# Joining wo to the down projection along K for token-tile pairs 0 to 6 instead of 1 to 5, with the last pair's products in two other PSUM banks

## Chip, cores, metric

One core of a Trainium2 chip. The metric is the device time of one execution in microseconds (us), lower is better. Engine names in the profile: PE is TensorE's matmuls, PEld its weight loads, DVE is VectorE, ACT is ScalarE, POOL is GpSimd, SP the engine that issues transfers.

## The reference

The output is a residual plus two branches of the same normalised input, for 2048 tokens of width 512:

```python
xn = layernorm(x)
# branch A: linear attention with softmax features, then a projection
o = num / den                       # 2048 x 512
a = o @ wo                          # 512 x 512
# branch B: gated bilinear unit
h = (xn @ w_gate) * (xn @ w_up)     # 2048 x 1792
b = h @ w_down                      # 1792 x 512
out = x + a + b
```

So `wo` and `w_down` both end in the same 512 output columns: `[h, o] @ [w_down; wo]` is one product with a longer K. This is what "joined along K" means.

## The kernel before

Tokens are handled in 8 pairs of 128-token tiles. For a pair the down projection is done by Strassen's scheme in Winograd's form: seven products of half size in place of eight. Each is 7 matmuls along K (half of 1792 is 7 x 128), 128 tokens by 256 columns. The operands are sums of blocks: GpSimd makes four sums of h for every pair (`S1` to `S4`), and the sums of the weights once. There are two forms of the step. The old one adds wo in the plain way:

```python
def DOWN_STEPS(p):                       # cut
    pa, pb = bank(4, 0, 256), bank(5, 0, 256)
    # P1 -> pa, P7 -> pb, P6 -> pa, P5 -> pa: 7 matmuls each
    mm(prod(pb, A22, T4, False) + wo_part(pb, t2, 0), name=f"P4.{p}")     # 7 + 4
    mm(prod(pa, S4, B22, False) + wo_part(pa, t1, 256), name=f"P3.{p}")   # 7 + 4
    mm(prod(d, A12, B21, True) + wo_part(d, t1, 0), name=f"P2.{p}")       # 7 + 4
    # W22: 4 more matmuls of wo in a bank of the ring; in the last pair in two halves
```

The joined form treats wo as two more K blocks of the same scheme, with sums of the attention output oT (`SOSUMS`, on GpSimd, four a pair) and of wo (`TOSUMS`, once):

```python
def CAT_STEPS(p):                        # cut
    def P(n, d, a_, b_, oa, ob, first, last):
        mm(prod(d, a_, b_, first, False), name=f"P{n}.{p}")               # 7
        mm([(d, oa[:, k, :], ob[:, k, :], False, last and k == 1) for k in range(2)],
           name=f"P{n}o.{p}")                                             # + 2
    # order P1 P2 P7 P6 P5 P4 P3; pa holds P1 P6 P5 P3, pb holds P2, then P7 P4
```

After each product VectorE reads the running sum out of the bank, so the next product in that bank has to wait for it. The order of instructions on every engine is fixed at build time by a list scheduler, which takes the first ready step in program order. Beside the pairs TensorE has 28 gate/up units for the last 512 tokens (8 matmuls of 256 columns each, in a ring of banks 0 to 3), and the feature and attention products of the q tiles.

The softmax here doesn't subtract the row's maximum and nothing guards it: scores larger than these inputs give would overflow.

Of the kernel before, what the change touches and what calls it, by code (L numbers as in the profile page):

```python
# [16 lines left out]
D = 512  # L17
# [342 lines left out]
PD = -1  # L360
PX = -1
SE = {}
UE = 1.6
QP0 = 1
QP1 = 2
# [2 lines left out]
TRQ = 1500.0  # L368
TRO = 800.0
PS = -1  # L370
CAT = (1, 2, 3, 4, 5)
SOE = POOL
TOE = POOL
PLN = 0
# [12 lines left out]
def _build(nc, es, A_x, A_wqkv, A_w_phi, A_wo, B_w_gate, B_w_up, B_w_down, out):  # L387
# [65 lines left out]
    def bank(b, lo=0, n=512):  # L453
        return psum[:, b * 512 + lo: b * 512 + lo + n]
# [67 lines left out]
    def group(o, pairs):  # L522
        n = len(pairs)
        return [(o, l, r, i == 0, i == n - 1) for i, (l, r) in enumerate(pairs)]
# [15 lines left out]
    def xnT(q, s_lo, n):  # L540
        return xnT_v[:, q, s_lo:s_lo + n]
# [250 lines left out]
    def hs(s_lo):  # L792
        return s_lo % 1536
# [76 lines left out]
    def BLOCK(kind, ft, ba):  # L870
# [58 lines left out]
                act_op(gslot(ft, 2), pa, name=f"ge{ft}.2", prio=PA)  # L929
        return [p1, p7, p6, p2, p4, p5, p3]  # L930

    def U2(ft, s_lo):
        b = nb()
        mm(group(bank(b, 0, 256), [(wg_v[:, q, ft * 128:(ft + 1) * 128], xnT(q, s_lo, 256)) for q in range(NQ)])
           + group(bank(b, 256, 256), [(wu_v[:, q, ft * 128:(ft + 1) * 128], xnT(q, s_lo, 256)) for q in range(NQ)]),
           name=f"gu{ft}.{s_lo}")
        g = gring()[:, 0:256]
        act_op(g, bank(b, 0, 256), name=f"ge{ft}.{s_lo}")
        h = hT_v[:, ft, hs(s_lo):hs(s_lo) + 256]
        dve(lambda e: e.tensor_tensor(out=h, in0=bank(b, 256, 256), in1=g, op=ALU.mult), [bank(b, 256, 256), g], [h],  # L940
            name=f"h{ft}.{s_lo}")

    def GU2(fts, s_lo, bg, bu, order):
# [48 lines left out]
    def NUM(t):  # L992
        nv = numb()
        mm([(nv[:, c, 0:68], qT_v[:, t % NQT, c, :], kvbd_v[:, c, :], True, True) for c in range(8)], name=f"n{t}")
        sm = qsum_v[:, t % 5, :].rearrange("p (c h s) -> p c h s", c=8, s=2)[:, :, :, 0]
        w = qw_v[:, t % 4, :]
        wv4 = w.rearrange("p (c h) -> p c h", c=8)
        den = nv[:, :, 64:68]
        dve(lambda e: e.scalar_tensor_tensor(out=wv4, in0=sm, scalar=1e-6, in1=den, op0=ALU.mult, op1=ALU.add),
            [qsum_v[:, t % 5, :], den], [w], cost=210.0, name=f"nd{t}")  # L1000
        dve(lambda e: e.reciprocal(out=w, in_=w), [w], [w], cost=360.0, name=f"nr{t}")  # L1001
        o = oslot(t)
        ov = o.rearrange("p (c h d) -> p c h d", c=8, h=4)
        src = nv[:, :, 0:64].rearrange("p c (h d) -> p c h d", h=4)
        dve(lambda e: e.tensor_tensor(out=ov, in0=src, in1=wv4[:, :, :, None].to_broadcast([128, 8, 4, 16]),  # L1005
                                      op=ALU.mult), [src, w], [o], cost=600.0, name=f"no{t}")
        dst = oT_v[:, t % 4, :, :]
        sc.dma(SP, dst, o, 131072, turn=True, reads=[o], writes=[dst], name=f"oT{t}").reserve = TRO
# [17 lines left out]
    def hA(half, t):  # L1026
        s = hs(t * 128)
        return hT_v[:, half * HF:(half + 1) * HF, s:s + 128]

    def SSUMS(p):  # L1030
        assert ui[0] >= (10 if p < 2 else NA2 if p < 6 else NA2 + (14, 28)[p - 6])
        S1, S2, S3, S4 = (S_v[:, p % 2, w] for w in range(4))
        A11, A12, A21, A22 = hA(0, 2 * p), hA(1, 2 * p), hA(0, 2 * p + 1), hA(1, 2 * p + 1)
        e3, e1, e2, e4 = (DVE if c == "D" else POOL for c in SE.get(p, "PPPP"))
        sums(e3, S3, A11, A21, ALU.subtract, f"S3.{p}", 0)
        sums(e1, S1, A21, A22, ALU.add, f"S1.{p}", 0)
        sums(e2, S2, S1, A11, ALU.subtract, f"S2.{p}", 0)
        sums(e4, S4, A12, S2, ALU.subtract, f"S4.{p}", 0)

    To_v = sbv("x", 12 * 512, 4 * 512).bitcast(F16).rearrange("p (w k j) -> p w k j", w=4, k=2)  # L1040
    So_v = sbv("vext", 0, 2 * 4 * 256).bitcast(F16).rearrange("p (r w k s) -> p r w k s", r=2, w=4, k=2)
# [37 lines left out]
    def DOWN_STEPS(p):  # L1079
        t1, t2 = 2 * p, 2 * p + 1  # L1080
        final = p == NT // 2 - 1
        S1, S2, S3, S4 = (S_v[:, p % 2, w] for w in range(4))
        A11, A12, A22 = hA(0, t1), hA(1, t1), hA(1, t2)
        pa, pb = bank(4, 0, 256), bank(5, 0, 256)
        t11, t21, t22 = (tf_v[:, p % 2, w] for w in range(3))

        def o(t, c):
            return sbv("ostg", (t % 4) * 512 + c * 256, 256)

        def x(t, c):  # L1090
            return x_res(t)[:, c * 256:(c + 1) * 256]

        def s1():
            mm(prod(pa, A11, B11, True), name=f"P1.{p}")
            post(p, t11, pa, x(t1, 0), "t11")

        def s2():
            mm(prod(pb, S3, T3, True), name=f"P7.{p}")
            post(p, t22, pb, x(t2, 1), "t22")

        def s3():
            mm(prod(pa, S2, T2, False), name=f"P6.{p}")
            post(p, t21, pa, x(t2, 0), "t21")

        def s4():
            mm(prod(pa, S1, T1, False), name=f"P5.{p}")
            post(p, t22, pa, t22, "t22b")

        def s5():
            mm(prod(pb, A22, T4, False) + wo_part(pb, t2, 0), name=f"P4.{p}")  # L1110
            post(p, o(t2, 0), pb, t21, "c21")
            if p == NT // 2 - 1:
                store(t2, 0, 256)

        def s6():
            mm(prod(pa, S4, B22, False) + wo_part(pa, t1, 256), name=f"P3.{p}")
            post(p, o(t1, 1), pa, x(t1, 1), "c12")
            if p == NT // 2 - 1:
                store(t1, 256, 256)

        def s7():
            d = bank(nb(), 0, 256) if final else pb
            mm(prod(d, A12, B21, True) + wo_part(d, t1, 0), name=f"P2.{p}")
            post(p, o(t1, 0), d, t11, "c11")
            store(t1, 0, 256 if p == NT // 2 - 1 else 512)

        def s8():
            w = 128 if final else 256
            for lo in range(0, 256, w):
                d = bank(nb(), 0, w)  # L1130
                mm([(d, oT_v[:, t2 % 4, q, :], wo_v[:, q, 256 + lo:256 + lo + w], q == 0, q == NQ - 1)
                    for q in range(NQ)], name=f"W22.{p}")
                oo, tt = o(t2, 1)[:, lo:lo + w], t22[:, lo:lo + w]
                dve(lambda e, oo=oo, d=d, tt=tt: e.tensor_tensor(out=oo, in0=d, in1=tt, op=ALU.add), [d, tt], [oo],
                    cost=60.0 + 1.045 * w, name=f"c22.{p}.{lo}")
            if final:
                store(t2, 256, 256, ACT)
            else:
                store(t2, 0, 512)
        if final:  # L1140
            return [s1, s2, s3, s4, s7, s5, s6, s8]
        return [s1, s2, s3, s4, s5, s6, s7, s8]

    def CAT_STEPS(p):
# [2 lines left out]
        S1, S2, S3, S4 = (S_v[:, p % 2, w] for w in range(4))  # L1147
        O1, O2, O3, O4 = (So_v[:, p % 2, w] for w in range(4))
        R1, R2, R3, R4 = (To_v[:, w] for w in range(4))
        A11, A12, A22 = hA(0, t1), hA(1, t1), hA(1, t2)  # L1150
        pa, pb = bank(4, 0, 256), bank(5, 0, 256)
        t11, t21, t22 = (tf_v[:, p % 2, w] for w in range(3))

        def o(t, c):
# [8 lines left out]

        def s1():
            P(1, pa, A11, B11, oA(0, t1), oB(0, 0), True, False)
            post(p, t11, pa, x(t1, 0), "t11")

        def s2():
            P(2, pb, A12, B21, oA(1, t1), oB(1, 0), True, True)
            post(p, o(t1, 0), pb, t11, "c11")  # L1170

        def s3():
            P(7, pb, S3, T3, O3, R3, True, False)
# [15 lines left out]
        def s7():  # L1189
            P(3, pa, S4, B22, O4, oB(1, 1), False, True)  # L1190
            post(p, o(t1, 1), pa, x(t1, 1), "c12")
            store(t1, 0, 512)
        return [s1, s2, s3, s4, s5, s6, s7, lambda: None]

    one = nc.const_aps.tensor(1.0, [128, 512], BF16)

# [48 lines left out]
    rest = [(U, f, sg) for ft in range(NB, NF // 2) for f in (ft, ft + NF // 2) for sg in (1, 2)]  # L1245
    units += rest
    NA2 = len(units)
    units += [(U2, ft, s_lo) for s_lo in (1536, 1792) for ft in range(NF)]
    ui = [0]

    def nextU():
        if ui[0] < len(units):
# [44 lines left out]
    assert ui[0] >= NA  # L1297
    load_x(SP, 4, 4, name="rx")
    load_x(SP, 8, 4, name="rx")
    down = DOWN_STEPS(0)  # L1300
    nextU()
    KVS(NT, 1)
    KVX()
    ring_banks[0] = [0, 1, 2, 3]
    rp[0] = 0
    nextU()
    down[0]()
    down[1]()
    NUM(0)
    nextU()  # L1310
    SSUMS(1)
    nextU()
    NUM(1)
    TOSUMS(TOE)
    u0 = ui[0]
    n_left = len(units) - u0
    NP = NT // 2
    for p in range(NP):
        def some(fr):
            k = int(round(u0 + n_left * min(1.0, (p + fr) / (NP - UE))))  # L1320
            while ui[0] < min(k, len(units)):
                nextU()
        a, b = 2 * p + 2, 2 * p + QA
        if p == 2:
            load_x(SP, 12, 4, name="rx", slot=0)
        def Qs(pos):
            for k, at in ((0, QP0), (1, QP1)):
                if at == pos and b + k < NT:
                    Q(b + k)
        if p > 0:  # L1330
            down = CAT_STEPS(p) if p in CAT else DOWN_STEPS(p)
            Qs(0)
            down[0]()
            some(0.1)
            Qs(1)
            down[1]()
# [8 lines left out]
        some(0.4)  # L1345
        Qs(3)
        down[3]()
        if 2 <= p + 1 < NP:
            SSUMS(p + 1)
        if a + 1 < NT:  # L1350
            NUM(a + 1)
# [7 lines left out]
        some(0.8)  # L1359
        down[6]()  # L1360
        some(1.0)
        down[7]()

    assert ui[0] == len(units)
    sc.chain("P6.7 P2.7 P5.7 P4.7 P3.7")

    for st in sc.steps:
        if st.eng in (ACT, DVE, POOL) and not isinstance(st.lane, tuple) and st.idx > late[0]:
# [40 lines left out]
```

## Time and profile before

| | before |
|---|---|
| median of 3 runs | 211.93 us (211.37 to 212.01) |
| span of the core in the profiled run | 209.8 us |
| PE busy | 204.5 us, 97% |
| GpSimd busy | 169.6 us, 81% |
| weight loads (one a matmul, all recorded) | 1620 |

How to read it: the page gives each engine's busy time and share. PE's ends are modelled, so 97% alone does not show that it never waits. The lines themselves stand in the prediction below.

### The profile page before, as it was taken

Reading aid. Unit: us, or ns where it says so; the run is one execution under the profiler, and the core shown is the slowest. Engines: PE = TensorE matmul, PEld = TensorE weight load, DVE = VectorE, ACT = ScalarE, POOL = GpSimd, SP = SyncE. Lnnn points to the kernel's source line nnn. Section 1 sums busy time; section 2 is a strip of 40 time slices with the busy share of each in tenths; the row PEclk is TensorE's granted clock in tenths of the full one; section 3 lists DMA queues with packets and bytes.
Section 4 is the critical chain, followed back from the end, with each engine's and each line's share of the span. In section 5 each row is a group of like instructions: output and inputs, shape, how many; then the busy total and the mean of one; then the engine's idle time right before and its main releaser. Section 6 shows DMA issues by size and latency. Waiting matters only on the chain.

```text
span 209.8 us, 4274 instructions
## 1 busy us (share of the span) xinstructions
PE 204.5 (97%) x1603; PEld 136.3 (65%) x1620; DVE 158.7 (76%) x307; ACT 113.3 (54%) x293; POOL 169.6 (81%) x215
## 2 busy tenths in 40 slices
PE   8999999999999999999999999999999999999995
PEld 3875444444454444454456797988978888799884
DVE  4857799998966797989987875948659486695743
ACT  4756999698796959697822613416144251531000
POOL 4061698439999999999999999999999989990540
PEclk9999999999999999999999999999999999999999
DMA  5999924964100000222521135183351705635211
GB/s 161 334 264 355 245 59 96 327 137 140 32 18 0 3 0 0 50 52 53 197 54 28 25 78 125 34 174 101 70 129 25 175 13 115 80 75 128 50 52 50
DMA packets 50244, 21.52 MB, mean 103 GB/s; under 512 B 37424, under 2 KB 50224, under 8 KB 50224
## 3 DMA queue, kind: packets, MB, share of 16 engines
q1 hardware_dynamic: 49552, 20.93, 40.5%
q10 hardware_dynamic: 672, 0.33, 0.6%
q8 instruction: 12, 0.20, 0.4%
q14 instruction: 8, 0.07, 0.1%
HBM read 10.24 MB, written 2.10 MB: 59 GB/s over the span
## 4 chain that ended last, share of the span: by engine, by line
PE 80%; POOL 7%; ACT 5%; DMA 3%; DVE 2%; issue 1%; DVEq 0%
PE ps L510 78%; ACT arena L463 5%; POOL arena L781 4%; DMA arena<-arena 3%; PE ps L1199 2%; POOL arena L731 2%; POOL arena L636 1%; DVE arena L781 1%; DVE arena L722 1%; POOL arena L729 0%; DVE arena L756 0%; ACT ps L463 0%; DVE arena L940 0%; DVE arena L1071 0%; DVEq L349 0%
## 5 line engine op out<-in xcount | busy, mean ns | idle before, releaser
L510 PE MATMUL ps<-arena 128*128 128x256 bf16 (+5 forms) x1593 | 200.3, 286 | 1.9 <-ACT ps L463 0.4
L510 PEld LDWEIGHTS ps<-arena 128*128 128x128 bf16 (+1 forms) x1610 | 135.0, 98 | 67.8 <-ACT arena L463 2.0
L781 POOL TENSOR_TENSOR arena<-arena 128x256 f16<-128x256 bf16 (+3 forms) x120 | 124.3, 1060 | 12.9 <-DVE arena L940 7.4
L463 ACT ACTIVATE arena<-ps 128x512 bf16<-128x512 f32 (+3 forms) x168 | 83.4, 533 | 67.9 <-PE ps L510 64.7
L722 DVE TENSOR_REDUCE arena<-arena 128x64 f32<-128x1024 bf16 x32 | 38.6, 1208 | 1.0 <-ACT arena L463 0.9
L1071 DVE TENSOR_TENSOR arena<-ps,arena 128x256 bf16<-128x256 f32 (+1 forms) x56 | 23.3, 422 | 17.4 <-PE ps L510 16.1
L463 ACT ACTIVATE arena<-arena 128x64 f32<-128x64 f32 (+4 forms) x96 | 28.4, 314 | 12.2 <-DVE arena L722 8.8
L731 POOL TENSOR_TENSOR arena<-arena 128x512 bf16<-128x512 bf16 x32 | 33.8, 1060 | 0.4
L940 DVE TENSOR_TENSOR arena<-ps,arena 128x256 f16<-128x256 f32 x30 | 12.4, 420 | 11.3 <-ACT arena L463 9.7
L862 DVE TENSOR_TENSOR arena<-ps,arena 128x512 f16<-128x512 f32 x24 | 16.1, 683 | 1.0 <-PE ps L510 0.8
L811 DVE TENSOR_TENSOR arena<-ps,arena 128x512 f16<-128x512 f32 x14 | 9.5, 684 | 4.9 <-PE ps L510 3.5
L756 DVE TENSOR_TENSOR arena<-ps,arena 128x512 bf16<-128x512 f32 x16 | 10.8, 683 | 2.1 <-ACT arena L463 1.5
L627 DVE BATCH_NORM_STATS2 arena<-arena 128x6 f32<-128x512 bf16 x16 | 10.5, 673 | 2.1 <-DMA arena<-in_A_x_dram 2.0
L868 DVE TENSOR_TENSOR ps<-ps,arena 128x512 f32<-128x512 f32 x12 | 8.2, 696 | 4.3 <-PE ps L510 3.0
L1005 DVE TENSOR_TENSOR arena<-ps,arena 128x512 bf16<-128x512 f32 x16 | 11.0, 685 | 0.3
L729 POOL TENSOR_TENSOR arena<-arena 128x32 f32<-128x32 f32 x32 | 8.3, 262 | 3.5 <-ACT arena L463 3.4
L609 POOL TENSOR_TENSOR arena<-arena 128x128 bf16<-128x128 bf16 x4 | 1.6, 428 | 8.7 <-DMA arena<-in_A_w_phi_dram 8.7
L636 POOL TENSOR_SCALAR arena<-arena 128x1 f32<-128x1 f32 x12 | 3.3, 290 | 6.0 <-ACT arena L463 6.0
L868 DVE TENSOR_TENSOR arena<-ps,arena 128x512 bf16<-128x512 f32 x12 | 8.0, 680 | 0.0
L463 ACT ACTIVATE ps<-ps 128x512 f32<-128x512 f32 x12 | 7.2, 600 | 0.0
L1001 DVE RECIPROCAL arena<-arena 128x32 f32<-128x32 f32 x16 | 5.6, 352 | 0.5
L1199 PE MATMUL ps<-const-bfloat16-1.0 128*128 128x512 bf16 x10 | 4.4, 626 | 0.8 <-PEq L1394 0.8
(22 smaller groups left out, 26.6 us busy)
## 6 DMA issues: line engine op xcount, KB each, us to landing
arena<-in_A_x_dram SPq DMA_DIRECT2D x6, 512.0 KB, 5.2
arena<-in_B_w_down_dram SPq DMA_DIRECT2D x1, 1792.0 KB, 7.6
out_dram<-arena SPq DMA_DIRECT2D x14, 128.0 KB, 2.0
arena<-in_B_w_gate_dram SPq DMA_DIRECT2D x1, 768.0 KB, 7.9
arena<-in_B_w_up_dram SPq DMA_DIRECT2D x1, 768.0 KB, 8.4
arena<-arena SPq DMA_TRANSPOSE x44, 2.5
arena<-in_B_w_gate_dram SPq DMA_DIRECT2D x2, 256.0 KB, 4.4
arena<-in_B_w_gate_dram SPq DMA_DIRECT2D x1, 512.0 KB, 6.1
```

The costliest lines, as they stand in the source:

```text
L463: return e.activation(out=out_ap, in_=in_ap, func=func, scale=scale, **kw)
L510: ins = e.matmul(o, lhsT=l, rhs=r, start=s, stop=p, skip_group_check=True)
L627: dve(lambda e, t=t: e.bn_stats(stats_v[:, t, :], x_tile(t)), [x_tile(t)], [stats_v[:, t, :]], cost=600.0, name=f"st{t}", win=win, prio=prio)
L722: dve(lambda e, ei=ei, so=so: e.tensor_reduce(out=so, in_=ei.rearrange("p (h f) -> p h f", f=16), axis=AX.X, op=ALU.add), [ei], [so], cost ...
L731: pool(lambda e: e.tensor_tensor(out=ev[:, :, 1, :], in0=ev[:, :, 1, :], in1=ratio[:, :, None].to_broadcast([128, H, 16]), op=ALU.mult), [ ...
L756: dve(lambda e: e.tensor_tensor(out=o1, in0=src, in1=rp_[:, :, :, None].to_broadcast([128, 8, 4, 16]), op=ALU.mult), [src, rs_v[:, t % 4, ...
L781: fn = lambda e: e.tensor_tensor(out=out_, in0=a_, in1=b_, op=op)
L862: dve(lambda e: e.tensor_tensor(out=h, in0=src, in1=g, op=ALU.mult), [src, g], [h], name=f"h{ft}.{sg}", prio=PD)
L868: dve(lambda e: e.tensor_tensor(out=o, in0=src, in1=sn, op=ALU.add), [src, sn], [o], name=name, prio=PD)
L940: dve(lambda e: e.tensor_tensor(out=h, in0=bank(b, 256, 256), in1=g, op=ALU.mult), [bank(b, 256, 256), g], [h], name=f"h{ft}.{s_lo}")
L1005: dve(lambda e: e.tensor_tensor(out=ov, in0=src, in1=wv4[:, :, :, None].to_broadcast([128, 8, 4, 16]), op=ALU.mult), [src, w], [o], cost=6 ...
L1071: dve(lambda e: e.tensor_tensor(out=out_, in0=in_ps, in1=in_sb, op=ALU.add), [in_ps, in_sb], [out_], cost=328.0, name=f"{name}.{p}")
```

## The change

The intent is to save the matmuls that the plain form of wo costs more, in two more pairs, and to give the last pair's first products banks that are free before pair 6 is done. The core of the diff:

```diff
-CAT = (1, 2, 3, 4, 5)
+CAT = (0, 1, 2, 3, 4, 5, 6)
+AB = {7: (2, 3)}
 ...
-        pa, pb = bank(4, 0, 256), bank(5, 0, 256)
+        pa, pb = (bank(b, 0, 256) for b in AB.get(p, (4, 5)))
 ...
-    down = DOWN_STEPS(0)
+    down = CAT_STEPS(0) if 0 in CAT else DOWN_STEPS(0)
 ...
-    down[0]()
-    down[1]()
+    if 0 not in CAT:
+        down[0]()
+        down[1]()
     NUM(0)
 ...
     TOSUMS(TOE)
+    if 0 in CAT:
+        SOSUMS(0, SOE)
+        SSUMS(1)
+        down[0]()
+        down[1]()
 ...
+        if p in AB:
+            ring_banks[0] = [0, 1]
```

The rest adds settings that are off (other orders, Strassen blocks for the gate/up units at count 0) and exchanges the halves of a bank in which the late gate/up units keep gate and up.

More of the change, by code (lines that the diff above doesn't have):

```diff
@@ L362 @@
 SE = {}
+SED = 'PPPP'
+SLATE = ()
+P2B = ()
+AB = {7: (2, 3)}
+CO = {}
+CH = "P6.7 P2.7 P5.7 P4.7 P3.7"
+NX = 0
+ZP = 0
+WSE = POOL
+XSE = POOL
+PB = -1
+NRA = ()
+SD = ()
+SPL = ((0, 7),)
 UE = 1.6
@@ L930, in BLOCK @@
         return [p1, p7, p6, p2, p4, p5, p3]
+    Tz_v = xnT_v[:, :, 0:512].bitcast(F16).rearrange("p w (k s) -> p w k s", k=2)
+    zw = [sbv("Wp", NQ * 512, 1024), sbv("Wp", NQ * 512 + 1024, 1024), sbv("wv", NQ * 512 - 1024, 1024)]
+    zw = [v.bitcast(F16).rearrange("p (w k j) -> p w k j", w=4, k=2) for v in zw]
+    zs = sbv("sums", 0, 1024).bitcast(F16).rearrange("p (r s) -> p r s", r=4)
+    zg = sbv("gring", 0, 4 * 512).rearrange("p (r s) -> p r s", r=8)
+    zc = {"w": 0, "s": 0, "g": 0}
@@ new lines, in _build, with zB, ZXSUMS, ZWSUMS @@
+    zgate = {}
+    zW = {}
+    def zB(k, c):
+        return xnT_v[:, 2 * k:2 * k + 2, 1536 + c * 256:1792 + c * 256]
+    def ZXSUMS():
+        X1, X2, X3, X4 = (Tz_v[:, w] for w in range(4))
+        for n, (o_, a_, b_) in enumerate(((X1, zB(0, 1), zB(0, 0)), (X3, zB(1, 1), zB(0, 1)), (X2, zB(1, 1), X1),
+                                          (X4, zB(1, 0), X2))):
+            sums(XSE, o_, a_, b_, ALU.subtract, f"Xz{n}", 0)
+    def ZWSUMS(kind, ft):
+        zW[kind, ft] = zw[zc["w"] % 3]
+        zc["w"] += 1
+        S1, S2, S3, S4 = (zW[kind, ft][:, w] for w in range(4))
+        A = lambda i, k: wA(W_v[kind], i, k, ft)
+        sums(WSE, S3, A(0, 0), A(1, 0), ALU.subtract, f"{kind}z3.{ft}", 0)
+        sums(WSE, S1, A(1, 0), A(1, 1), ALU.add, f"{kind}z1.{ft}", 0)
+        sums(WSE, S2, S1, A(0, 0), ALU.subtract, f"{kind}z2.{ft}", 0)
+        sums(WSE, S4, A(0, 1), S2, ALU.subtract, f"{kind}z4.{ft}", 0)
@@ new lines, in zsnap, with zgslot, ZBLOCK, S @@
+    def zsnap():
+        zc["s"] += 1
+        return zs[:, zc["s"] % 4, :]
+    def zgslot(f, c):
+        zc["g"] += 1
+        zgate[f, c] = zg[:, zc["g"] % 8, :]
+        return zgate[f, c]
+    def ZBLOCK(kind, ft):
+        ft2 = ft + NF // 2
+        A = lambda i, k: wA(W_v[kind], i, k, ft)
+        X1, X2, X3, X4 = (Tz_v[:, w] for w in range(4))
+        st = {}
+        nm = f"z{kind}.{ft}"
+        def S(w):
+            return zW[kind, ft][:, w]
+        def take(k):
+            st[k + "i"] = nb(True)
+            st[k] = bank(st[k + "i"], 0, 256)
+            return st[k]
+        def free(k):
+            held.discard(st[k + "i"])
+        def zadd(o_, a_, b_, n):
+            dve(lambda e: e.tensor_tensor(out=o_, in0=a_, in1=b_, op=ALU.add), [a_, b_], [o_], cost=328.0,
+                name=n + nm, prio=PB)
+        def done(f, c, src):
+            if kind == "g":
+                act_op(zgslot(f, c), src, name=f"ge{nm}", prio=PB)
+                return
+            h = hT_v[:, f, hs(1536 + c * 256):hs(1536 + c * 256) + 256]
+            g = zgate[f, c]
+            dve(lambda e: e.tensor_tensor(out=h, in0=src, in1=g, op=ALU.mult), [src, g], [h], cost=328.0,
+                name=f"h{nm}", prio=PB)
+        def p1():
+            pa = take("a")
+            xprod(pa, A(0, 0), zB(0, 0), True, "b1" + nm)
+            seed(take("c"), pa, "sd" + nm)
+        def p7():
+            pb = take("b")
+            xprod(pb, S(2), X3, True, "b7" + nm)
+            st["p7"] = zsnap()
+            act_op(st["p7"], pb, name="s7" + nm, prio=PB)
+        def p2():
+            xprod(st["c"], A(0, 1), zB(1, 0), False, "b2" + nm)
+            done(ft, 0, st["c"])
+            free("c")
+        def p6():
+            xprod(st["a"], S(1), X2, False, "b6" + nm)
+            st["u2"] = zsnap()
+            act_op(st["u2"], st["a"], name="s2" + nm, prio=PB)
+        def p4():
+            pb = st["b"]
+            xprod(pb, A(1, 1), X4, False, "b4" + nm)
+            if kind == "g":
+                zadd(zgslot(ft2, 0), pb, st["u2"], "a4")
+            else:
+                zadd(pb, pb, st["u2"], "a4")
+                done(ft2, 0, pb)
+            free("b")
+        def p5():
+            xprod(st["a"], S(0), X1, False, "b5" + nm)
+            if kind == "g":
+                zadd(zgslot(ft2, 1), st["a"], st["p7"], "a5")
+            else:
+                pt = bank(nb(), 0, 256)
+                zadd(pt, st["a"], st["p7"], "a5")
+                done(ft2, 1, pt)
+        def p3():
+            xprod(st["a"], S(3), zB(1, 1), False, "b3" + nm)
+            done(ft, 1, st["a"])
+            free("a")
+        return [p1, p7, p2, p6, p4, p5, p3]
@@ L932, in U2 @@
     def U2(ft, s_lo):
         b = nb()
-        mm(group(bank(b, 0, 256), [(wg_v[:, q, ft * 128:(ft + 1) * 128], xnT(q, s_lo, 256)) for q in range(NQ)])
-           + group(bank(b, 256, 256), [(wu_v[:, q, ft * 128:(ft + 1) * 128], xnT(q, s_lo, 256)) for q in range(NQ)]),
+        GLO = 256 if s_lo >= 1536 else 0
+        mm(group(bank(b, GLO, 256), [(wg_v[:, q, ft * 128:(ft + 1) * 128], xnT(q, s_lo, 256)) for q in range(NQ)])
+           + group(bank(b, 256 - GLO, 256), [(wu_v[:, q, ft * 128:(ft + 1) * 128], xnT(q, s_lo, 256)) for q in range(NQ)]),
@@ L936, in U2 @@
            name=f"gu{ft}.{s_lo}")
         g = gring()[:, 0:256]
-        act_op(g, bank(b, 0, 256), name=f"ge{ft}.{s_lo}")
+        act_op(g, bank(b, GLO, 256), name=f"ge{ft}.{s_lo}")
         h = hT_v[:, ft, hs(s_lo):hs(s_lo) + 256]
-        dve(lambda e: e.tensor_tensor(out=h, in0=bank(b, 256, 256), in1=g, op=ALU.mult), [bank(b, 256, 256), g], [h],
+        dve(lambda e: e.tensor_tensor(out=h, in0=bank(b, 256 - GLO, 256), in1=g, op=ALU.mult), [bank(b, 256 - GLO, 256), g], [h],
             name=f"h{ft}.{s_lo}")
@@ L1000, in NUM @@
             [qsum_v[:, t % 5, :], den], [w], cost=210.0, name=f"nd{t}")
-        dve(lambda e: e.reciprocal(out=w, in_=w), [w], [w], cost=360.0, name=f"nr{t}")
+        if t in NRA:
+            recip(w, w, f"nr{t}")
+        else:
+            dve(lambda e: e.reciprocal(out=w, in_=w), [w], [w], cost=360.0, name=f"nr{t}")
         o = oslot(t)
@@ L1030, in SSUMS @@
     def SSUMS(p):
-        assert ui[0] >= (10 if p < 2 else NA2 if p < 6 else NA2 + (14, 28)[p - 6])
+        assert ui[0] >= (10 if p < 2 else NA2 if p < 6 else (NA3, len(units))[p - 6])
         S1, S2, S3, S4 = (S_v[:, p % 2, w] for w in range(4))
         A11, A12, A21, A22 = hA(0, 2 * p), hA(1, 2 * p), hA(0, 2 * p + 1), hA(1, 2 * p + 1)
-        e3, e1, e2, e4 = (DVE if c == "D" else POOL for c in SE.get(p, "PPPP"))
-        sums(e3, S3, A11, A21, ALU.subtract, f"S3.{p}", 0)
-        sums(e1, S1, A21, A22, ALU.add, f"S1.{p}", 0)
-        sums(e2, S2, S1, A11, ALU.subtract, f"S2.{p}", 0)
-        sums(e4, S4, A12, S2, ALU.subtract, f"S4.{p}", 0)
+        es = [DVE if c == "D" else POOL for c in SE.get(p, SED)]
+        for (n, o_, a_, b_, op), eng in zip(((3, S3, A11, A21, ALU.subtract), (1, S1, A21, A22, ALU.add),
+                                             (2, S2, S1, A11, ALU.subtract), (4, S4, A12, S2, ALU.subtract)), es):
+            for lo, hi in SPL if eng == POOL else ((0, HF),):
+                sums(eng, o_[:, lo:hi], a_[:, lo:hi], b_[:, lo:hi], op, f"S{n}.{p}" + (f".{lo}" if lo else ""), 0)
     To_v = sbv("x", 12 * 512, 4 * 512).bitcast(F16).rearrange("p (w k j) -> p w k j", w=4, k=2)
@@ L1121, in s7 @@
         def s7():
-            d = bank(nb(), 0, 256) if final else pb
+            d = bank(nb(), 0, 256) if final or p in P2B else pb
             mm(prod(d, A12, B21, True) + wo_part(d, t1, 0), name=f"P2.{p}")
@@ L1149, in CAT_STEPS @@
         R1, R2, R3, R4 = (To_v[:, w] for w in range(4))
+        cb = []
         A11, A12, A22 = hA(0, t1), hA(1, t1), hA(1, t2)
-        pa, pb = bank(4, 0, 256), bank(5, 0, 256)
+        pa, pb = (bank(b, 0, 256) for b in AB.get(p, (4, 5)))
         t11, t21, t22 = (tf_v[:, p % 2, w] for w in range(3))
@@ L1165, in s1 @@
             P(1, pa, A11, B11, oA(0, t1), oB(0, 0), True, False)
-            post(p, t11, pa, x(t1, 0), "t11")
-        def s2():
-            P(2, pb, A12, B21, oA(1, t1), oB(1, 0), True, True)
-            post(p, o(t1, 0), pb, t11, "c11")
+            if p in SD:
+                cb.append(nb(True))
+                seed(bank(cb[0], 0, 256), pa, f"sd11.{p}")
+            else:
+                post(p, t11, pa, x(t1, 0), "t11")
+        def s2():
+            if p in SD:
+                d = bank(cb[0], 0, 256)
+                P(2, d, A12, B21, oA(1, t1), oB(1, 0), False, True)
+                post(p, o(t1, 0), d, x(t1, 0), "c11")
+                held.discard(cb[0])
+                return
+            d = bank(nb(), 0, 256) if p in P2B else pb
+            P(2, d, A12, B21, oA(1, t1), oB(1, 0), True, True)
+            post(p, o(t1, 0), d, t11, "c11")
         def s3():
@@ L1192, in s7 @@
             store(t1, 0, 512)
-        return [s1, s2, s3, s4, s5, s6, s7, lambda: None]
+        order = CO.get(p, "1276543")
+        f = {"1": s1, "2": s2, "7": s3, "6": s4, "5": s5, "4": s6, "3": s7}
+        return [f[c] for c in order] + [lambda: None]
     one = nc.const_aps.tensor(1.0, [128, 512], BF16)
@@ L1247, in _build, with weight @@
     NA2 = len(units)
-    units += [(U2, ft, s_lo) for s_lo in (1536, 1792) for ft in range(NF)]
+    std = [ft for ft in range(NF) if ft % (NF // 2) >= NX]
+    units += [(U2, ft, 1536) for ft in std]
+    blocks = [(kind, ft) for ft in range(NX) for kind in "gu"]
+    for i, b in enumerate(blocks):
+        units += [(f,) for f in ZBLOCK(*b)]
+        if i + 3 < len(blocks):
+            units.append((ZWSUMS,) + blocks[i + 3])
+    NA3 = len(units)
+    units += [(U2, ft, 1792) for ft in std]
     ui = [0]
+    def weight(u):
+        return 4 if u[0] is U2 or u[0] is U else 0 if u[0] is ZWSUMS else 1
     def nextU():
@@ L1306, in _build @@
     nextU()
-    down[0]()
-    down[1]()
+    if 0 not in CAT:
+        down[0]()
+        down[1]()
     NUM(0)
     nextU()
-    SSUMS(1)
+    if 0 not in CAT:
+        SSUMS(1)
     nextU()
@@ L1314, in _build @@
     TOSUMS(TOE)
+    if 0 in CAT:
+        SOSUMS(0, SOE)
+        SSUMS(1)
+        down[0]()
+        down[1]()
+    cum = [0]
+    for u in units[ui[0]:]:
+        cum.append(cum[-1] + weight(u))
     u0 = ui[0]
-    n_left = len(units) - u0
     NP = NT // 2
@@ L1319, in some @@
         def some(fr):
-            k = int(round(u0 + n_left * min(1.0, (p + fr) / (NP - UE))))
-            while ui[0] < min(k, len(units)):
+            k = cum[-1] * min(1.0, (p + fr) / (NP - UE))
+            while ui[0] < len(units) and cum[ui[0] - u0] + weight(units[ui[0]]) / 2 <= k:
                 nextU()
+        if p == ZP and NX:
+            ZXSUMS()
+            for b_ in blocks[:3]:
+                ZWSUMS(*b_)
         a, b = 2 * p + 2, 2 * p + QA
@@ L1347, in _build @@
         down[3]()
-        if 2 <= p + 1 < NP:
+        if 2 <= p + 1 < NP and p + 1 not in SLATE:
             SSUMS(p + 1)
@@ L1361, in _build @@
         some(1.0)
+        if p + 1 in SLATE:
+            SSUMS(p + 1)
         down[7]()
     assert ui[0] == len(units)
-    sc.chain("P6.7 P2.7 P5.7 P4.7 P3.7")
+    sc.chain(CH)
     for st in sc.steps:
```

## The prediction

> **What bounds the kernel now.** I read the page first, then the waits of TensorE, the groups by form, the busy time by stretch, and last the chain of waits and the timelines of the end. The top of the page says which engine the time belongs to:
>
> ```profile
> span 209.8 us, 4274 instructions
> PE 204.5 (97%) x1603; PEld 136.3 (65%) x1620; DVE 158.7 (76%) x307; ACT 113.3 (54%) x293; POOL 169.6 (81%) x215
> PE   8999999999999999999999999999999999999995
> POOL 4061698439999999999999999999999989990540
> PEclk9999999999999999999999999999999999999999
> ```
>
> TensorE (PE) is occupied nearly everywhere at a full clock; GpSimd (POOL) is full from slice 10 to slice 36, and has holes only in the last four slices. A busy PE could still hide waits, so the next question is what PE waited for:
>
> ```profile
> PE ps L1199 <- PEq L1394: 0.8, 1, 0.8
> PE ps L510 <- ACT ps L463: 0.4, 1, 0.4
> PE ps L510 <- DVE arena L868: 0.3, 1, 0.3
> PE ps L510 <- issue: 0.2, 1, 0.2
> PE ps L510 <- ACT arena L463: 0.2, 1, 0.2
> ```
>
> Columns: who waited for whom, total us, times, longest. That is 1.9 us in the whole run, and none of it in the part that the change touches. The chain of waits (start us, length us, what) confirms it:
>
> ```profile
> 179.22 0.05 issue
> 179.27 27.60 PE ps L510 x267
> 206.87 0.02 issue
> 206.89 0.42 DVE arena L1071
> 207.31 0.20 DVE arena L1134
> 207.51 0.20 DVEq L349
> ```
>
> From 57 us on the chain is PE alone, back to back; after its last product there are about 2.5 us of last additions and the last store. So in the down-projection stage (about 109 to 207 us) the time is the number of matmuls times the spacing of one, as long as nothing makes PE wait. The spacing comes from a stretch that holds only 256-column matmuls (columns: window, length, busy us and count for PE, PEld, DVE, ACT, POOL, clock, DMA share, GB/s):
>
> ```profile
> 190.00:197.00 7.00, 7.00 (x78) 6.32 (x77) 4.78 (x14) 1.15 (x3) 0.91 (x1) 1.00 0.39 94
> 197.00:206.00 9.00, 9.00 (x85) 8.05 (x83) 4.61 (x11) 0.00 (x0) 4.74 (x3) 1.00 0.18 53
> ```
>
> Every matmul has one weight load, and all 1620 weight loads are recorded while some matmul records are missing; so 9.00 us / 83 = 108.4 ns a matmul. By counting weight loads in program order I also matched them to the products: product P6 of the last pair takes 7 matmuls in 0.75 us, P2 with its four of wo 1.2 us for 11, which is the same spacing.
>
> **What the Trainium skill says.** "TensorE: Matmul & The Clock Gate", Back-to-back issue gap, gives N/2.4 + 2.5 ns for a warm stream: 109.2 ns at N = 256. The trace agrees (108.4). "PSUM — Partial Sum Buffer", Terms, says that two engines on one bank at once are an error, so each read of an accumulator by VectorE must be a wait for the next product in that bank; the trace shows the length of this turn: P1 of pair 6 ends at 191.33, its VectorE read runs 191.64 to 192.07, so about 0.8 us with the signal back. "GPSIMD Engine Reference", 3.1 Elementwise, puts a two-input elementwise at about 2.6 cycles an element, which at 1.2 GHz is 2.2 ns; here 896 elements take 1883 ns (2.1 ns) and 256 take 673 ns (a fixed part shows), so it agrees roughly and I use the durations. "DMA: Bandwidth & Descriptors", Anatomy of one DMA, has about 2.0 us fixed; the transposes that bring the attention output oT take 2.3 us from issue to landing.
>
> **The change, part by part.** *TensorE.* Both forms do seven half-size products (Strassen's scheme) of 7 matmuls along K, 49 in all. The old form adds wo plainly: 4 matmuls in P4, P3 and P2 and a block W22 of 4, so 16, total 65. The joined form adds two matmuls to each product: 14, total 63. Two fewer a pair, two pairs (0 and 6): 4 x 108.4 ns = **0.43 us less** PE work. Pair 7 stays in the old form.
>
> *VectorE.* The old form has 8 additions a pair, the joined 7: two fewer of about 0.42 us, 0.84 us, beside PE.
>
> *GpSimd.* Each newly joined pair needs four sums of oT:
>
> ```profile
> L781 POOL TENSOR_TENSOR arena<-arena 128x896 f16<-128x896 f16 x32 | 60.1, 1883 | 11.3 <-DVE arena L940 7.4 <-DMA arena<-arena 3.4 <-PE ps L510 0.2
> L781 POOL TENSOR_TENSOR arena<-arena 128x256 f16<-128x256 bf16 x55 | 36.2, 673 | 1.5 <-DMA arena<-in_B_w_up_dram 1.4
> ```
>
> 8 x 0.67 = 5.4 us more, 2.7 at pair 0 and 2.7 at pair 6. The four sums of wo (1.16 us each) exist already, but pair 0 now needs them, and they move ahead of the sums of pair 1.
>
> *Pair 0.* Its old P1 and P7 ran at 109.1 to 110.5 without oT. Now P1 and P2 come first, P7 third, and every product has an oT part. oT of tile 0 landed at 114.82, of tile 1 at 118.77. GpSimd can then give the four sums between about 119 and 123; the old P4 of this pair ran at 120.7 and the pair ended at 125.8, so the need is at about the same time. Gate/up units stand ready as other PE work (28 of them, 8 matmuls or 0.87 us each, none bound to this pair's oT). The 2.7 us push back the GpSimd queue, but what it pushes is early: the second sum for pair 2 is done at 129.3 and its product runs near 148; the sums of pair 6 are done at 183 and used from 193. The short margin is the sums of oT of pair 1 (third sum done 133.0, used 133.6), which are placed ahead of the large sums in the queue. I count 0.
>
> *Pair 6.* Its sums of oT wait for tile 13, landed at 189.97; GpSimd sits idle there:
>
> ```profile
> 187.59 1.06 POOL L731 TENSOR_TENSOR arena<-arena 128x512 bf16<-128x512 bf16 x1
> 196.09 5.80 POOL L781 TENSOR_TENSOR arena<-arena 128x896 f16<-128x896 f16 x3 [7.45 <-DVE arena L940]
> ```
>
> (start us, length us, engine, line, ..., idle before). Four sums fit from 190 to 193 in the 7.45 us hole, before the sums of pair 7 at 196.1. I count 0 if they don't slip.
>
> *The other banks.* Joined pair 6 has P2 and P7 in one bank, with a VectorE read between, and P6 and P5 in the other: two turns of 0.8 us which need other PE work. After the last gate/up unit (194.86) only one small attention product and pair 7 are left. In banks 4 and 5 the first two products of pair 7 would have to wait for pair 6; in banks 2 and 3 they can be that filler (2 x 0.76 us). So the bank change mostly keeps the 0.43 us from being lost; by itself it can save nothing, since PE does not wait there today.
>
> *The rest of the diff* (new knobs, Z blocks at zero count, gate and up halves of a bank exchanged in the late units) changes no number of instructions.
>
> Sum: 211.93 - 0.43 = **211.5 us**.
>
> **The rivals.** *A. GpSimd becomes the bound.* For: it is at 81%, full for two thirds of the run, and gets 5.4 us. If the 2.7 us at pair 0 were passed on, the time would be up to 211.9 + 2.3 = 214.2. Against: PE waits for it nowhere after 109 us but at a margin of 10 us and more for the large sums, and from 170 us on it has small holes that absorb the delay. *B. A new wait in the last pairs.* The second sum of pair 7 is done at 199.9 and its product starts at 201.47, a margin of 1.5 us; with 0.43 us less PE work before it, 1.1 us is left. If the sums of pair 6's oT, or a gate/up unit run later by 1 us, eat this, PE waits and the gain is gone: 211.9 to 212.5. For: this is where fillers are few. *C. More than the count.* If the exchange of banks and order also removed small waits, 210.8; against: 0.05 us pieces of "issue" every ten us are all that the chain shows to remove, plus one turn at the very end that stays.
>
> **Range and chances.** The central value is C's neighbour, the plain count. The runs of before spread from 211.37 to 212.01, as much as the whole effect, so the range is 0.7 us either side: 210.8 to 212.2, with B inside and A outside. Two per cent is 4.2 us, ten times the gain: faster 0.01, same 0.97, slower 0.02 (A at its worst plus a wait at the end).
>
> **What would show it.** The changed profile should have 1616 weight loads, two VectorE additions fewer, 219 to 223 GpSimd instructions (8 more) and about 175 us of it; PE's waits still near 1.9 us; the span about 0.4 us shorter, all of it between 109 and 207 us; the 7.45 us hole of GpSimd split in two around a group of four sums of 256; P1 and P7 of pair 7 mixed into pair 6. I am wrong on A if PE shows waits for POOL from 115 to 135 us; on B if one appears after 195 us; and if the weight loads fall by 4 with the spacing unchanged and the span does not follow, the price was a wait that the views must name.

## The result, and the profile after

| | before | changed |
|---|---|---|
| median | 211.97 us, 6 runs (211.01 to 212.22) | 210.95 us, 6 runs (210.67 to 211.42) |
| span of the profiled run | 209.8 us | 209.6 us |
| weight loads | 1620 | 1616 |
| VectorE / GpSimd instructions | 307 / 215 | 305 / 223 |

The ratio is 0.9963, 95% interval 0.9939 to 0.9988. Ratios here are the mean time of one kernel's fast runs over that of the other's of the same rounds, so not quite the ratio of the medians. The class is "same", as forecast, and the time lies inside the stated range; but the ratio means 0.8 us, and the prediction had worked out 0.43. The experiments ask which of the two is the change.

The top of the page after:

```profile
span 209.6 us, 4281 instructions
PE 205.6 (98%) x1616; PEld 136.3 (65%) x1616; DVE 158.5 (76%) x305; ACT 113.9 (54%) x293; POOL 174.5 (83%) x223
PE   8999999999999999999999999999999999999995
POOL 4070598439999999999999999999999999997640
```

The instruction counts moved exactly as the two forms say. PE's busy time went up although it has four matmuls fewer: this trace has every matmul record (1616), that of before lacks 17, so busy PE is not to be compared between the two. GpSimd is now full up to slice 36 and its holes at the end are smaller. What PE waited for, and the end of the chain of waits (start us, length us, what):

```profile
PE ps L1345 <- PEq L1568: 0.8, 1, 0.8
PE ps L524 <- ACT ps L477: 0.4, 1, 0.4
PE ps L524 <- DVE arena L882: 0.3, 1, 0.3
```

```profile
57.45 149.26 PE ps L524 x1252
206.71 0.02 issue
206.73 0.42 DVE arena L1203
207.15 0.20 DVE arena L1266
207.35 0.20 DVEq L349
```

No wait is new, and the chain from 57 us on is one piece of PE. The weight loads say the same more sharply; the timeline of PEld from 107 us on has one row, before and after, which means no idle time of 150 ns or more until the last product (columns: start, length, engine, line, operation, out<-in, count, idle time before):

```profile
106.91 100.21 PEld L510 LDWEIGHTS ps<-arena 128*128 128x128 bf16 x952
```

```profile
107.14 99.83 PEld L524 LDWEIGHTS ps<-arena 128*128 128x128 bf16 x950 [0.32 <-DVE arena L770]
```

So where did the time come from? All weight loads are recorded in both traces, so counting them in program order names every product; the start and end times of single products below were found in this way. I take as **the stage** the stretch from the end of the last k-v product (the last thing that both programs have in the same place on PE: the first 200 steps on PE are the same, and so are the first 40 transfers that SP issues) to the end of the last wo block. As windows of before, and of the changed kernel (length first, then busy us and counts for PE, PEld, DVE, ACT, POOL):

```profile
109.15:207.12 97.97, 97.65 (x928) 82.12 (x930) 67.21 (x150) 29.85 (x79) 83.92 (x77) 1.00 0.37 80
```

```profile
109.42:206.96 97.54, 97.54 (x931) 81.73 (x927) 66.96 (x148) 30.29 (x79) 88.77 (x85) 1.00 0.39 80
```

97.97 against 97.54: 0.43 us, the four matmuls. The counts in these two lines include the records that straddle the window's edges. The profiled run of the changed kernel reached the stage 0.27 us later (109.42 against 109.15), in a part where the programs do not differ; that is why the two spans differ by only 0.2 us.

### The profile page after: what moved, and what is told of

The parts are those of the page before. It is cut to its first block, busy times and chain, and to the rows that moved or that the text cites. A ratio compares the mean times of both kernels' runs of the same rounds, so it can differ in the third digit from the quotient of the medians.

```text
span 209.6 us, 4281 instructions
## 1 busy us (share of the span) xinstructions
PE 205.6 (98%) x1616; PEld 136.3 (65%) x1616; DVE 158.5 (76%) x305; ACT 113.9 (54%) x293; POOL 174.5 (83%) x223
## 4 chain that ended last, share of the span: by engine, by line
PE 81%; POOL 7%; ACT 5%; DMA 3%; DVE 2%; issue 1%; DVEq 0%
PE ps L524 79%; ACT arena L477 5%; POOL arena L795 4%; DMA arena<-arena 3%; PE ps L1345 2%; POOL arena L745 2%; DVE arena L795 1%; POOL arena L650 1%; DVE arena L736 1%; POOL arena L743 0%; ACT ps L477 0%; DVE arena L1203 0%; DVEq L349 0%; DVE arena L1266 0%; ACT arena L773 0%
## 5 line engine op out<-in xcount | busy, mean ns | idle before, releaser
L795 POOL TENSOR_TENSOR arena<-arena 128x256 f16<-128x256 bf16 (+3 forms) x128 | 129.4, 1034 | 7.5 <-DMA arena<-arena 3.4
```

The costliest lines, as they stand in the source:

```text
L795: fn = lambda e: e.tensor_tensor(out=out_, in0=a_, in1=b_, op=op)
```

## The experiments

Theory A: the change is worth its four matmuls, and the new banks are what keeps this from being lost to waits. Theory B: something beyond the count gained, since the timed runs show about 0.8 us. A third view, a rival of both: GpSimd is so near its bound that its extra sums decide. The stage is measured in each profiled run, beside the timed ratio with its interval. Each run had 5 rounds, with the kernel before run beside it. All outputs were correct.

### 1. The changed kernel again, twice

No edit. First:

> The changed kernel once more, unaltered. If the saving is only the four matmuls (theory A: 4 x 108.4 ns = 0.43 us), the ratio to before is about 0.998 and its interval should hold 0.998; in the trace the stretch from the end of the last k-v product (kv15) to the end of the last wo block is 0.4 to 0.5 us shorter than before's, and what differs ahead of kv15 is run to run. If something beyond the count helped (theory B, since the medians on record differ by 1.0 us), the ratio is 0.995 again and the stretch after kv15 is shorter by 0.8 us or more.

Measured: 211.11 us against 211.84, ratio 0.9958 (0.9932 to 0.9984). The stage is 97.54 us, before it 109.04. And:

> The changed kernel a third time, beside the one above on the same chip. The stretch after kv15 should be 97.54 us again; the timed ratio to before, 0.9963 and 0.9958 so far, should hold 0.998 in its interval if the count is all there is; a third value near 0.996 with an interval that leaves 0.998 out would mean that something outside that stretch gained too.

Measured: 211.16 us against 211.82, ratio 0.9958 (0.9922 to 0.9993). The stage is 97.54 us once more.

The stage repeats to 0.01 us, so there theory A holds to the digit. But the timed ratio stayed near 0.996 three times. Each of the three intervals still holds 0.998, near its upper end (0.9988, 0.9984, 0.9993); weighted together, as an estimate from the three, they give 0.9960 with 0.0016 either side, which leaves 0.998 out. To see what the timed runs add, I split each run's time into the core's span and the rest, as each run records both, and compare only the two calls in which both kernels ran side by side with their spans on record. Before, 22 runs: mean 211.96 us = span 209.87 + 2.09 outside it. Changed, 12 runs: 211.15 = 209.31 + 1.84. The difference of the spans is 0.56 us, with a scatter of 0.47 and 0.41 us for single runs, which makes about 0.31 us of uncertainty: it fits 0.43. The other 0.25 us lies outside the span, where none of the kernel's instructions run. There the time has two levels: about 1.8 us, or 2.0 to 3.5. Of before 10 of the 22 runs were above 2 us, of the changed kernel 1 of 12, and none of the six in the table above. That this follows from the change is not shown: with only pair 0 joined it was 5 of 6 runs, with no pair joined 1 of 6, which follows no order that I can see. So theory B falls inside the program; why the time outside it differed stays open.

### 2. Pair 0 alone, and pair 6 alone

```diff
-CAT = (0, 1, 2, 3, 4, 5, 6)
-AB = {7: (2, 3)}
+CAT = (0, 1, 2, 3, 4, 5)       # r_pair0
+AB = {}
```

```diff
-CAT = (0, 1, 2, 3, 4, 5, 6)
+CAT = (1, 2, 3, 4, 5, 6)       # r_pair6
```

> Only pair 0 joined in addition (pairs 0 to 5), last pair in banks 4 and 5 as before. Theory A: two matmuls fewer, 0.22 us less than before, no new PE wait from 109 to 135 us. Rival (GpSimd): the 2.7 us of extra sums and the wo sums moved ahead make PE wait at pair 0: slower than before by up to 2 us. Theory B would put more than 0.22 us here.

> Only pair 6 joined in addition (pairs 1 to 6), with the last pair in banks 2 and 3. Theory A: two matmuls fewer, 0.22 us less than before, 0.22 us more than the changed kernel; no PE wait after 190 us. Theory B would put more than 0.22 us here.

Measured, pair 0 first and then pair 6:

```profile
108.58:206.33 97.75, 97.75 (x932) 81.87 (x928) 67.14 (x149) 30.27 (x79) 85.87 (x80) 1.00 0.41 80
```

```profile
109.22:206.97 97.75, 97.75 (x932) 81.90 (x928) 67.02 (x149) 29.84 (x79) 86.52 (x81) 1.00 0.39 80
```

The stage is 97.75 us in both, 0.22 less than before, and no wait is new. The timed ratios, 0.9998 (0.9968 to 1.0027) and 0.9998 (0.9970 to 1.0026), cannot see a tenth of a per cent. Each pair gives its two matmuls and nothing else.

### 3. No pair joined

```diff
-CAT = (0, 1, 2, 3, 4, 5, 6)
+CAT = ()
```

> No pair joined, last pair in banks 2 and 3: 1630 matmuls, 10 more than before and 14 more than the changed kernel. If the count is all that the joining is worth, the stretch after kv15 is 97.97 + 10 x 0.108 = 99.05 us, and the timed ratio to before about 1.005. Rival: joining costs waits elsewhere, so undoing all of it costs less than that: under 98.6 us.

Measured: 212.63 us against 211.61, ratio 1.0051 (1.0023 to 1.0078); the stage as a window:

```profile
109.17:208.23 99.06, 98.75 (x938) 83.06 (x940) 68.43 (x155) 30.13 (x79) 71.97 (x57) 1.00 0.39 79
```

99.06 us, where 99.05 was expected: ten matmuls more than before are ten spacings, with 12 us less of GpSimd work in the stage (71.97 against 83.92 busy) making no difference at all. This is the strongest support for the count, as the lever is larger than what a run scatters.

### 4. The banks alone, and the change without them

```diff
-CAT = (0, 1, 2, 3, 4, 5, 6)
+CAT = (1, 2, 3, 4, 5)          # r_banksonly: banks 2 and 3 kept
```

> The bank change alone: pairs 1 to 5 joined as before, the last pair in banks 2 and 3. The prediction says it can save nothing by itself, as TensorE does not wait there: equal to before, and 97.97 us from the end of kv15 to the last wo block, as before (within 0.05). Rival: part of what the timed runs gained beyond the four matmuls comes from the banks: 0.3 us or more less in that stretch.

Measured: ratio 1.0028 (0.9994 to 1.0061), stage 97.97 us, the same as before:

```profile
109.22:207.19 97.97, 97.66 (x928) 82.07 (x930) 67.21 (x150) 29.83 (x79) 83.89 (x77) 1.00 0.38 80
```

The banks alone save nothing. This kernel also has the rest of the diff (the halves of a bank exchanged, the settings that are off), so the two together are worth nothing in the stage.

```diff
-AB = {7: (2, 3)}
+AB = {}                        # r_oldbanks: pairs 0 to 6 joined, banks 4 and 5
```

> Pairs 0 to 6 joined, but the last pair's products back in banks 4 and 5. Theory A with the turn of a bank: pair 6 now has no other PE work between P4o and P3 (a wait of about 0.6 us), P1 of pair 7 and P6 of pair 7 wait for reads in bank 4 (0.1 and 0.4 us), and a half of the last wo block is spent as filler so that the kernel ends on P3 and a 256-wide addition: 1.1 to 1.5 us more than the changed kernel, so 0.7 to 1.1 us slower than before. Rival: the fillers that are left are enough and the bank move does nothing: equal to the changed kernel.

Measured: 212.93 us against 211.84, ratio 1.0031 (1.0002 to 1.0061), slower than before. The timeline of PEld in the last 20 us:

```profile
189.97 8.03 PEld L524 LDWEIGHTS ps<-arena 128*128 128x128 f16 x85
198.58 2.96 PEld L524 LDWEIGHTS ps<-arena 128*128 128x128 f16 x31 [0.58 <-DVE arena L1203]
201.78 5.03 PEld L524 LDWEIGHTS ps<-arena 128*128 128x128 f16 x47 [0.24 <-DVE arena L1203]
```

The first stop is P3 of pair 6, which waits until VectorE has read P5 out of the same bank; the second is P6 of pair 7, waiting for the read of P1. In the changed kernel P1 of pair 7 runs at the first place and P3, P3o and P7 at the second. The expected stops were 0.6, 0.1 and 0.4 us; they were 0.58, 0.03 and 0.24. The stage is 98.15 us, 0.61 more than the changed kernel's, and from there to the end it takes 2.84 us in place of 2.65, as the kernel now ends on P3 and a 256-wide addition. Together 0.81 us: less than the 1.1 to 1.5 expected, since the stops were shorter and the 7 matmuls after each of the two long ones took 0.66 us in place of 0.75, but almost twice the 0.43 that the joining saves. So without the banks the change would have been a loss, of 0.38 us by the trace. The timed means differ by more, 212.76 against 212.01; of these 0.75 us only 0.23 is span and 0.52 lies outside it, so the loss inside the program rests on the trace.

### 5. More work for GpSimd

Sums of the same size into an unused buffer, in two places:

```diff
+    def DUMMY(p, n, tag):       # n groups of four sums of oT into the spent half of Wp
+        ...
         SOSUMS(0, SOE)
+        DUMMY(0, 2, "a")        # r_pool0
 ...
                 SOSUMS(p + 1, SOE)
+                if p + 1 == 6:
+                    DUMMY(6, 2, "b")   # r_pool6
```

> The changed kernel with eight more GpSimd sums of the same size into an unused buffer, right behind the four of pair 0: 5.4 us more GpSimd work at 121 us, twice over what joining pair 0 cost. If the large sums really have 10 us and more of margin, and the scheduler places other PE work ahead, the stretch after kv15 stays at 97.54 us (within 0.2). Rival (GpSimd nearly the bound): 1 to 5 us more, with PE waiting for POOL or for transposes of q between 125 and 150 us.

Measured: 212.1 us against 211.61, ratio 1.0029 (0.9982 to 1.0076), stage 98.25 us, 0.71 more than the changed kernel's. Theory A's "within 0.2" missed. The timelines of PEld and of GpSimd show the place:

```profile
145.20 1.29 PEld L524 LDWEIGHTS ps<-arena 128*128 128x128 f16 x17 [0.45 <-POOL arena L795]
146.66 55.03 PEld L524 LDWEIGHTS ps<-arena 128*128 128x128 f16 x527 [0.18 <-POOL arena L795]
201.94 5.58 PEld L524 LDWEIGHTS ps<-arena 128*128 128x128 f16 x55 [0.24 <-POOL arena L795]
```

```profile
144.48 1.29 POOL L795 TENSOR_TENSOR arena<-arena 128x256 f16<-128x256 bf16 x2 [0.99 <-DMA arena<-arena]
```

At the first two stops it is not the large sums that came late: the last two matmuls of P7 and of P6 of pair 2 waited for sums of oT. GpSimd itself stood idle for 0.99 us before the first of these, waiting for oT of tile 5. The extra sums had pushed back GpSimd's part of the q features (qp4 from 124.2 to 127.3), these their transposes, these the attention products (n5 from 133.5 to 137.1; TensorE shows no wait there, as the scheduler had given them a later place at build time), and so oT; tile 5 landed at 144.41 in place of 138.88, 1.6 us of it in the transfer itself (4.08 us from issue to landing in place of 2.47). The thin margin is this loop of GpSimd, transfer, TensorE, VectorE and transfer back to GpSimd, one turn a pair. The 2.7 us that the change itself adds at this place fit in it; twice that on top do not. The large sums of pair 2 still came in time, but with little left: the second was done at 143.49 for a product at 145.32, 1.8 us where the changed kernel has 9.4.

The third stop, at 201.94, is a large sum: P6 of pair 7 waits for the second sum of its pair, done at 201.89 in place of 199.66. GpSimd was busy for all of 150 to 190 us (40.00 of 40.00) and had not worked off its delay. So 0.24 us of this loss is GpSimd's own queue, as the rival has it.

Of the two slowest runs of this kernel (213.7 and 214.24 us) the first is the profiled one, and its profile shows another cause: the last two stores landed 3.5 and 3.3 us after their issue, where the changed kernel's take 1.5. The other run left no trace, so its cause is not shown.

> The changed kernel with eight more such sums behind the four of pair 6: 5.4 us more at 193 us, where the hole left in GpSimd is 2.9 us and the second sum of pair 7 has 1.6 us of margin before its product. So about 0.9 us of PE wait before P6 of pair 7, part of it filled with half of the last wo block, and a slightly longer end: 0.6 to 1.2 us more than the changed kernel. Rival: the margin is larger than read, no change; or GpSimd is the true bound at the end and all 5.4 us less the hole show, 2.5 us.

Measured: 211.67 us against 211.61, ratio 1.0002 (0.9973 to 1.0032), stage 97.54 us: no loss, against 0.6 to 1.2 expected.

```profile
109.26:206.80 97.54, 97.17 (x924) 81.72 (x927) 67.03 (x149) 30.25 (x79) 93.47 (x93) 1.00 0.37 80
```

GpSimd has 93.47 us of work in a stage of 97.54 here. My estimate had the delay too long: queued back to back the twelve sums took 7.5 us (0.63 each, where the four alone take 0.70), so the second sum of pair 7 ended 1.8 us later (92.04 us into the stage against 90.24), and the scheduler moved half of the last wo block (0.28 us) in front of P6, which then began without a wait. The margin of 1.6 us and the filler together were just enough.

### 6. The last pair joined too

If two matmuls fewer are worth 0.22 us a pair, the last pair is the next one to try.

```diff
-CAT = (0, 1, 2, 3, 4, 5, 6)
+CAT = (0, 1, 2, 3, 4, 5, 6, 7)
-                SOSUMS(p + 1, SOE)
+                SOSUMS(p + 1, DVE if p + 1 == 7 else SOE)
 # last pair: order P1 P6 P7 P5 P4 P3 P2, P2 in two halves of 128 columns in two banks,
 # c11 and the last store follow them
```

> The last pair joined as well: its four wo sums on VectorE, its products in the order P1 P6 P7 P5 P4 P3 P2, and P2 last in two halves of 128 columns in two banks, so that the end stays short. Count: the changed kernel's last pair is 49 + 12 matmuls of 256 and 8 of 128; this has 54 of 256 and 18 of 128. With 108.4 ns and about 56 ns: 61 x 0.1084 + 8 x 0.056 = 7.06 against 54 x 0.1084 + 18 x 0.056 = 6.86, so 0.20 us less. If no wait is added, the stretch after kv15 is 97.34 us. Rival: P6 of the last pair now comes one product earlier and its sum S2, or the sums of oT of tile 15, come too late: a wait of up to 1 us, and the end is later than the changed kernel's.

Measured: 212.16 us against 211.82, ratio 1.0014 (0.9979 to 1.0050); beside it the unaltered changed kernel took 211.16. The stage is 98.08 us, 0.54 more. The rival was right; timelines of PEld and of VectorE:

```profile
201.59 5.16 PEld L524 LDWEIGHTS ps<-arena 128*128 128x128 f16 x56 [0.85 <-DVE arena L795]
```

```profile
200.64 1.22 DVE L795 TENSOR_TENSOR arena<-arena 128x256 f16<-128x256 bf16 x4
```

oT of tile 15 landed at 200.11, its sums ran from 200.64, and P6o, the first user in this order, had to wait for the third until 201.59. The old form uses oT of tile 15 only from P4 on, 2.7 us after the start of P6 in the changed kernel. An order with P7 first and P2 in the middle would give the sums time, but then the end falls on a 256-wide addition again, which cost 0.19 us in experiment 4 and would eat the 0.20 gained (worked out, not run). I did not find a version that beats the changed kernel.

## Why the prediction was right, point by point

**The count.** Right: 4 x 108.4 ns = 0.43 us, and the stage went from 97.97 to 97.54. One pair is 0.22, seven pairs 1.52 (99.06 to 97.54). The spacing itself was read a little low, as the 83 of the window count a record that straddles its edge: from start to start the weight loads there are 109.2 ns apart, which makes 0.44.

**VectorE and GpSimd beside PE.** Right: two and eight instructions, about 5 us more GpSimd busy time in the stage (83.92 to 88.77), none of it in the time.

**Pair 0.** Right in its result. The sums of oT ran from 119.60 to 124.2 (119 to 123 expected), the pair ended at 127.6 in place of 125.8, and gate/up units filled PE in between. The margin of the large sums was put at 10 us and more: the second sum of pair 2 was done at 135.7 and its product ran at 145.1, so 9.4. (In the kernel before, the prediction had put this product near 148; the trace has it at 145.9, so its margin there was 16.6 us and not 18.7.) But experiment 5 shows that the argument looked at the wrong margin: what gives way first is the loop through q and oT, and a large sum only at the end. The prediction named the sums of oT as the short one, without the loop behind them.

**Pair 6.** Right in its result, wrong in a detail. The sums fit before those of pair 7, but the 7.45 us hole was not split in two:

```profile
189.07 1.06 POOL L745 TENSOR_TENSOR arena<-arena 128x512 bf16<-128x512 bf16 x1
190.11 2.79 POOL L795 TENSOR_TENSOR arena<-arena 128x256 f16<-128x256 bf16 x4
195.83 5.79 POOL L795 TENSOR_TENSOR arena<-arena 128x896 f16<-128x896 f16 x3 [2.92 <-DVE arena L1069]
```

GpSimd's queue was 1.5 us later here (189.07 against 187.59), the rest of what pair 0 had pushed back, so the sums follow without a gap and only the rear 2.92 us of the hole are left.

**The banks.** Right in both halves: alone they save nothing, and P1 and P7 of pair 7 became the filler (P1 at 198.78 between P4o and P3 of pair 6). The loss that they avert was larger than said: 0.81 us, not just the 0.43.

**The rivals.** A did not come; 5.4 us more at the same place bring 0.7 us of it, in part through the loop. B did not come either: its margin was worked out as 1.1 us and is 1.63 (199.66 to 201.29), because the last gate/up unit and with it the sums of pair 7 moved 0.2 to 0.3 us forward as well. C is empty: the 0.05 us pieces of "issue" are missing in this chain and present in that of the kernel of experiment 5 with the same stage of 97.54 us, so they are not time. The regular ones, every ten us or so, stand only in the five traces that lack 17 or 18 matmul records.

**The size of the total.** The term that the sum lacked is the time outside the span. The timed means differ by 0.81 us, of which 0.56 is span (0.43 fits) and the rest, 0.25, is outside, where the prediction assumed equality. What it depends on was not settled. So the mechanism of the sum was right, but that the median of 210.95 still lies in the range, 0.15 above its lower end, is owed to the width that the scatter of before had suggested; luck had a share in it. The range also did not hold all of rival B, as the prediction said: B ran to 212.5, the range to 212.2.

## What to carry to other kernels

When PE never waits in a stage, count matmuls times their spacing, and check it on a stage that the trace delimits exactly: here it repeats to 0.01 us, where the timed runs scatter by 0.4 to 0.6. A saved matmul is worth its time only if no wait takes its place, so look for the bank turns that the new order makes and for the independent products that can stand in them; here two free banks decided between a gain of 0.43 us and a loss of 0.38. A margin belongs to a loop and not to one engine's queue: follow a delay through transfers back to where it started before calling an engine's slack large.

## What the Trainium skill lacked or had wrong

- "TensorE: Matmul & The Clock Gate", Back-to-back issue gap, gives a sustained figure of about 131 ns a matmul at N = 512 for a stream of weight loads and matmuls, and says that the isolated formula over-counts there. Here, with one weight load for each matmul, 92 matmuls of 512 columns in a row start 215.8 ns apart (18.52 to 38.38 us of the changed kernel's trace), and those of 256 columns 109.2: the formula N/2.4 + 2.5 (215.8 and 109.2) holds for the stream as well.
- "Perfetto Trace Analysis", Per-engine timelines, says that the end of a matmul is estimated. It does not say what follows for reading waits: in the kernel with the old banks the wait shows as 0.30 us before PE and as 0.58 before PEld, and the second wait (0.24) not at all in PE's list. Waits of TensorE are to be read at the weight loads.
- The same page, Identifying the Most-Contended Engine, recommends the busy share of LDWEIGHTS, beside the share of peak FLOPs, to judge how close TensorE is to its limit. In the stage, where no wait of 150 ns shows, it was 84% (81.73 of 97.54): a load takes 98 ns and a 256-column matmul 109.2, so even a full stream of these reaches 90%.
- No page has the turn of a PSUM bank: from the end of a product's weight loads through a 256-column VectorE addition (0.42 us) to the next product there it is about 0.8 us (0.80 and 0.79 at the two stops of experiment 4).
- "DMA: Bandwidth & Descriptors", Anatomy of one DMA, gives a fixed cost, called about constant, for transfers that GpSimd issues; the section has none for stores that SP and ACT issue, nor their scatter. Here the last two stores, of 64 KB each and issued by SP or ACT, took 1.5 to 1.6 us from issue to landing in eleven traces and 3.5 and 3.3 in one, where the end after the last weight load takes 4.38 us in place of 2.65.
